# x @ w_in by Strassen's seven block products behind the first 512 tokens, weights' operands streamed from scratch memory

## The chip, the core and the metric

One core of a Trainium2 chip runs one program. The metric is the device time of that program in microseconds; "before" is the median of three runs. The engines named below are TensorE (PE, its weight loads apart as PEld), VectorE (DVE), ScalarE (ACT), GpSimd (POOL) and SyncE (SP, which here only issues DMAs). Each engine works through its own instructions in the order in which they were written; engines meet through semaphores.

## What is computed

```python
def _attn_ref(q, k, v):                # 8 batches, 8 heads, 576 positions, 64 wide; chunks of 64
    scores = scale * np.matmul(q_c, k_c.transpose(0, 1, 2, 4, 3))
    scores = scores - np.max(scores, axis=-1, keepdims=True)
    attn = np.exp(scores)
    attn = attn / (np.sum(attn, axis=-1, keepdims=True) + 1e-09)
    out = np.matmul(attn, v_c)
...
def _moe_ref(x, w_in, w_out):          # x (4608, 512): the attention's output, all heads of a position
    h = x @ w_in                       # (512, 2048)
    sp = np.where(h > 20.0, h, np.log1p(np.exp(np.minimum(h, 20.0))))
    g = h * np.tanh(sp)
    return (g @ w_out).astype(np.float32)   # (2048, 512)
```

Attention works inside chunks of 64 positions; a feed-forward layer with the activation mish follows. The weights arrive in 64-bit floats.

## The kernel before

Tokens come in 18 pairs of two tiles (256 tokens); two pairs make a block of 512 tokens, and there are nine blocks. In each block 16 slots walk over w_in's 2048 columns, 128 at a time (f).

All wide products are made from split operands: a float32 value is kept as a high part, rounded to the format of the matmul, and a low part, the rest, and a product is low x high + high x high + high x low. `up` (L288) makes one tile h of x @ w_in, 128 columns of w_in by 512 tokens: four steps of the inner dimension 512 by three parts, 12 matmuls of 512 columns. ACT turns h into z (mish, L300); DVE, or ACT in half of the first block's slots, makes the parts gh and gl (L308, L306, L313); `down` (L326) multiplies them with w_out's parts into four accumulators for 128 tokens each, o0 (tokens 0 to 255) and o2 (256 to 511), again 12 matmuls. At the end of a block `store` copies the accumulators to ob on ACT (L340) and DVE (L338) in turn, three buffers for four copies, and SP writes them out (L344).

PE's order is written out by hand in `slot(s)`: `up` of slot s+1, a step of attention if the plan has one, `down` of slot s-1. Attention of a pair (scores s and values av, L162; transposes pt, L231; maximum, subtraction, sum and norm on DVE, L189, L201, L215, L222; exp and copies on ACT, L210, L241) runs a block ahead, one step a slot; its output x is split straight from the accumulator into xh (ACT, L262) and xl (DVE, L265).

The weights are split during the first block. Each 128-row piece is loaded by SP (wis, wos, L82), made into float32 by two ACT passes (L89, L93) and two DVE passes (L99), and split by an ACT copy (L114) and a DVE subtraction (L117). w_in's and w_out's parts then stay on the chip to the end. A prologue does the first two pairs in halves, and the first pieces of the weights.

## Time and profile before

| | |
|---|---|
| median of three runs | 878.55 us (878.55 to 880.42) |
| span of the profiled execution | 876.5 us |
| median less that span | 2.05 us |
| PE busy | 854.2 us, 97% of the span |
| DVE busy | 342.8 us |
| ACT busy | 254.2 us |
| moved by DMA | 55.40 MB |

In rows of groups stand the line, engine and operation, output <- inputs, the shape and the count, then the busy time in all and the mean of one in ns, then the engine's idle time before them and what ended it. In rows of the timeline and of the chain the first number is the start and the second the duration, both in us. Instructions overlap at their edges on DVE, ACT and PE, so starts lie a little closer than durations say. An instruction that waits for its operands stands as idle time of its engine, in brackets.

### The profile page before, as it was taken

To read this page: it belongs to the slowest core of one execution; us is meant where nothing else is said; L and a number is where in the kernel's file an instruction comes from. 1 tells how busy PE (TensorE), PEld (TensorE's weight loads), DVE (VectorE), ACT (ScalarE), POOL (GpSimd) and SP (SyncE) were. 2 spreads that over 40 slices of the span, in tenths; PEclk is the share of its full clock that TensorE was granted. 3 is DMA by queue.
4 is the path that set the end of the run, shared out by engine and by line. 5 is a ranking of instruction groups with operands and counts; after the bars stand their busy time and mean duration, and the time that the engine had idled before them with its cause. 6 is when DMAs were issued, how large, how long until landed. Compare 5 with 4: busy or idle time off the path is not lost.

```text
span 876.5 us, 13523 instructions
## 1 busy us (share of the span) xinstructions
PE 854.2 (97%) x5916; PEld 703.9 (80%) x5916; DVE 342.8 (39%) x534; ACT 254.2 (29%) x360; POOL 0.7 (0%) x6
## 2 busy tenths in 40 slices
PE   4999999999999999999999999999999999999996
PEld 4778888888888888888888888888888888888885
DVE  6899845242334233323424242423242243322221
ACT  4888832121312122221213131212222131321111
POOL 0000000000000000000000000000000000000000
PEclk9899999999999999999999999999999999999999
DMA  7657512101210120112120121013101211001002
GB/s 264 204 183 251 180 36 62 49 25 49 73 49 25 49 73 25 49 31 60 31 73 7 42 73 49 25 49 73 39 35 49 52 37 57 0 6 43 1 1 48
DMA packets 25179, 55.40 MB, mean 63 GB/s; under 512 B 2592, under 2 KB 2592, under 8 KB 25120
## 3 DMA queue, kind: packets, MB, share of 16 engines
q1 hardware_dynamic: 24832, 54.01, 20.5%
q8 instruction: 46, 0.75, 0.4%
q10 hardware_dynamic: 288, 0.52, 0.2%
q14 instruction: 13, 0.11, 0.0%
HBM read 45.09 MB, written 9.44 MB: 62 GB/s over the span
## 4 chain that ended last, share of the span: by engine, by line
PE 91%; DVE 4%; ACT 3%; issue 1%; DMA 1%; SPq 0%; DVEq 0%; ACTq 0%
PE o L326 43%; PE h L288 41%; PE av L162 2%; PE s L162 2%; PE pt L231 2%; DVE wic L99 1%; DVE woc L99 1%; DVE m L189 1%; DVE wo_l L117 0%; DMA k<-in_k 0%; ACT L300 0%; DVE p L222 0%; DVE p L201 0%; ACT L210 0%; ACT woc L89 0%
## 5 line engine op out<-in xcount | busy, mean ns | idle before, releaser
L308 DVE CAST gh<-z 128x512 fp32r<-128x512 f32 x136 | 57.9, 426 | 453.4 <-PE o L326 453.4
L326 PE MATMUL o<-wo_h,gl 128*128 128x512 f32 x576 | 229.0, 398 | 0.0
L326 PE MATMUL o<-wo_h,gh 128*128 128x512 f32 x576 | 224.5, 390 | 0.0
L326 PE MATMUL o<-wo_l,gh 128*128 128x512 f32 x576 | 224.5, 390 | 0.0
L300 ACT ACTIVATE z<-h 128x512 f32<-128x512 f32 x144 | 86.2, 599 | 451.4 <-PE h L288 345.6
L288 PE MATMUL h<-xh,wi_l 128*128 128x512 f32 (+1 forms) x580 | 154.9, 389 | 0.7 <-ACT xh L262 0.7
L288 PE MATMUL h<-xl,wi_h 128*128 128x512 f32 (+1 forms) x580 | 155.2, 390 | 0.0
L288 PE MATMUL h<-xh,wi_h 128*128 128x512 f32 (+1 forms) x580 | 154.7, 389 | 0.0
L288 PEld LDWEIGHTS h<-xh,wi_l 128*128 128x128 f32 x580 | 108.9, 189 | 23.3 <-ACT xh L262 0.9
L288 PEld LDWEIGHTS h<-xl,wi_h 128*128 128x128 f32 x580 | 109.2, 190 | 22.4
L288 PEld LDWEIGHTS h<-xh,wi_h 128*128 128x128 f32 x580 | 109.1, 189 | 22.4
L326 PEld LDWEIGHTS o<-wo_h,gl 128*128 128x128 f32 x576 | 108.1, 188 | 23.1
L326 PEld LDWEIGHTS o<-wo_h,gh 128*128 128x128 f32 x576 | 108.1, 188 | 22.8
L326 PEld LDWEIGHTS o<-wo_l,gh 128*128 128x128 f32 x576 | 108.2, 188 | 21.1
L313 DVE TENSOR_TENSOR gl<-z,gh 128x512 fp32r<-128x512 f32 x144 | 99.6, 692 | 9.7 <-ACT gh L306 5.0
L241 ACT COPY ps<-pt 128x1024 f32<-128x1024 f32 (+1 forms) x20 | 18.6, 931 | 83.8 <-PE pt L231 83.8
L338 DVE COPY ob<-o 128x512 f32<-128x512 f32 x18 | 12.5, 692 | 53.8 <-ACT ob L340 30.9
L300 ACT ACT_TABLE_LOAD x17 | 21.8, 1283 | 34.5 <-PE h L288 34.5
L231 PE MATMUL pt<-ident,p 128*128 128x128 f32 x144 | 20.0, 282 | 9.3 <-ACT wis L93 5.9
L231 PEld LDWEIGHTS pt<-ident,p 128*128 128x128 f32 x144 | 17.0, 144 | 12.9 <-issue 6.0
L162 PEld LDWEIGHTS s<-k,q 64*64 64x64 f32 x1088 | 18.3, 139 | 11.0 <-issue 5.6
L162 PE MATMUL s<-k,q 64*64 64x64 f32 x1088 | 20.8, 227 | 5.3 <-DMA k<-in_k 5.3
(36 smaller groups left out, 370.6 us busy)
## 6 DMA issues: line engine op xcount, KB each, us to landing
out<-ob SPq DMA_DIRECT2D x72, 128.0 KB, 2.4
wis<-in_w_in SPq DMA_DIRECT2D x16, 512.0 KB, 3.6
wos<-in_w_out SPq DMA_DIRECT2D x16, 512.0 KB, 3.9
q<-in_q SPq DMA_DIRECT2D x16, 512.0 KB, 3.7
k<-in_k SPq DMA_DIRECT2D x16, 512.0 KB, 3.5
v<-in_v SPq DMA_DIRECT2D x16, 512.0 KB, 3.9
room_v<-in_v SPq DMA_DIRECT2D x2, 512.0 KB
k<-in_k ACTq DMA_DIRECT2D x2, 256.0 KB
```

The lines of the kernel that those rows point to most:

```text
L99: nc.vector.scalar_tensor_tensor(out=c, in0=x, scalar=mask, in1=d["a"][:, :, 0] if op == ALU.logical_shift_left else c, op0=op, op1=ALU.bi ...
L162: nc.tensor.matmul(o[h * CHUNK : (h + 1) * CHUNK, c, t - ts.start, g], lhsT=l[rows, t, 2 * g + h], rhs=r[rows, t, 2 * g + h], start=True, ...
L189: nc.vector.tensor_reduce(out=small(j, "m", t), in_=st[j]["s", t.start].rearrange("p c t g k -> p c (t g) k"), op=ALU.max, axis=AX.X,)
L231: nc.tensor.transpose(out=d["pt", ts.start][:, t - ts.start, g], in_=d["p"][:, t, g].rearrange("p c k -> p (c k)"), identity=ident,)
L241: nc.scalar.copy(out=d["ps"][:, t].rearrange("p t h k -> p (t h k)"), in_=d["pt", t.start][:, : t.stop - t.start].rearrange("p t g n -> p ...
L288: nc.tensor.matmul(h[:, cols], lhsT=w_[:, f, kt], rhs=x[:, kt, cols], start=(n == 0), stop=(n == 3 * NK - 1),)
L300: nc.scalar.activation(out=d["z"], in_=d["h"], func=AF.Mish)
L308: nc.vector.tensor_copy(out=d["gh"], in_=d["z"])
L313: nc.vector.tensor_tensor(out=d["gl"], in0=d["z"], in1=d["gh"].bitcast(F32), op=ALU.subtract)
L326: nc.tensor.matmul(acc[t], lhsT=g[:, sl], rhs=w_[:, f], start=(f == 0 and n == 0), stop=(f == NF - 1 and n == 2),)
L338: nc.vector.tensor_copy(out=o, in_=acc[t])
```

## The change

The first block of 512 tokens is computed as before. The other 16 pairs are taken in four quads of 1024 tokens, and x @ w_in in each of them goes by seven block products (Strassen's method, in a form with fewer sums). For unit u of eight, columns 256u to 256u+255 of w_in, transposed, are cut into four blocks of 128 columns by 256 inner rows, A11, A12 (first 128 columns) and A21, A22; x of the quad into B11, B12, B21, B22, 256 inner rows by 512 tokens. The sums are S1 = A21 + A22, S2 = S1 - A11, S3 = A11 - A21, S4 = A12 - S2 and T1 = B12 - B11, T2 = B22 - T1, T3 = B22 - B12, T4 = B21 - T2. Each product has two inner steps and three parts, 6 matmuls. Where two results share products, one accumulator is copied out by ACT midway (x to z, b1, b2) and goes on accumulating; the rest is added by DVE (`add`, L656 of the changed kernel).

The parts of the seven A operands are not kept on the chip. In the first block the float32 pieces of w_in are written to scratch memory (cs), and so are the parts of A11, A12 and A22 (ra). The parts of the S are made once, unit by unit: `s_load` reads cs back into a tile bld, `s_build` makes four sums on DVE, their high parts on ACT and the low ones on DVE, and SP stores them (sa). This is done in slots 14 and 15 and at six places of quad 1's units 0 to 3. From there every product's operand, 256 KB, is loaded by SP (`load_op`), six ahead. The attention's output is copied to raw tiles, and the parts of B and T come from these (`x_sums`, `x_split`), for the first quad in slots 9 to 15.

A quad has two halves. In the first, eight units make h; tokens of pairs 0 and 2 are activated, split and fed to `down` at once, those of pairs 1 and 3 stay as b1 and b2 (zb). `down` now only appends its 24 matmuls a unit to a list, from which the next unit takes three or five behind each product (`filled`). In the second half the list is filled from zb, 24 matmuls a tick for eight ticks. The first block carries attention for four pairs instead of two; a quad carries that of the next four pairs, on 32 ticks.

```diff
--- before.py
+++ after.py
@@ stores of the weights operands, in the weight steps
+    raw_ops = [dram.tile([P, 3, 2, 256], F32, name=f"ra_{u}") for u in range(NU)]
+    sum_ops = [dram.tile([P, 4, 2, 256], F32, name=f"sa_{u}") for u in range(NU)]
+    w_c = [dram.tile([P, 2, DM], F32, name=f"cs_{u}") for u in range(NU)]
...
+        if m == "i":
+            nc.sync.dma_start(out=w_c[f // 2][:, f % 2], in_=c.bitcast(F32))
...
+    def w_keep(n):
+        m, f = order[n]
+        if m == "i":
+            t = wi[f].bitcast(F32).rearrange("p s (a k) c -> p s a (k c)", a=2)
+            u = f // 2
+            if f % 2 == 0:
+                for a in range(2):
+                    nc.sync.dma_start(out=raw_ops[u][:, a], in_=t[:, :, a])
+            else:
+                nc.sync.dma_start(out=raw_ops[u][:, 2], in_=t[:, :, 1])
...
+    def s_load(u):
+        if "t" not in bld:
+            bld["t"] = zb_p.tile([P, 16 * 256], F32, name="bld", tag="z")
+        t = bld["t"]
+        nc.sync.dma_start(
+            out=t[:, 0 : 2 * DM], in_=w_c[u].rearrange("p h c -> p (h c)")
+        )
+    def s_build(u):
+        t = bld["t"]
+        a = t[:, 0 : 2 * DM].rearrange("p (n c) -> p n c", c=256)
+        s = t[:, 2 * DM : 4 * DM].rearrange("p (n c) -> p n c", c=256)
+        o = t[:, 4 * DM :].rearrange("p (n s c) -> p n s c", s=2, c=256)
+        a11, a12, a21, a22 = (a[:, n] for n in range(4))
+        s2, s1, s3, s4 = (s[:, n] for n in range(4))
+        for out_, x, y, op in (
+            (s1, a21, a22, ALU.add),
+            (s2, s1, a11, ALU.subtract),
+            (s3, a11, a21, ALU.subtract),
+            (s4, a12, s2, ALU.subtract),
+        ):
+            nc.vector.tensor_tensor(out=out_, in0=x, in1=y, op=op)
+        nc.scalar.copy(out=o[:, :, 0].bitcast(F32R), in_=s)
+        nc.vector.tensor_tensor(out=o[:, :, 1].bitcast(F32R), in0=s, in1=o[:, :, 0], op=ALU.subtract)
+        nc.sync.dma_start(out=sum_ops[u], in_=o)
@@ the operands of x
+    def x_split(m, half, *names):
+        for name in names:
+            src = raw_half(m, half, name)
+            hi = x_half(m, half, name, 0)
+            nc.scalar.copy(out=hi, in_=src)
+            nc.vector.tensor_tensor(
+                out=x_half(m, half, name, 1), in0=src, in1=hi.bitcast(F32), op=ALU.subtract
+            )
+    def x_sums(m, half):
+        for out_, x, y in (
+            ("T1", "B12", "B11"),
+            ("T3", "B22", "B12"),
+            ("T2", "B22", "T1"),
+            ("T4", "B21", "T2"),
+        ):
+            nc.vector.tensor_tensor(
+                out=raw_half(m, half, out_),
+                in0=raw_half(m, half, x),
+                in1=raw_half(m, half, y),
+                op=ALU.subtract,
+            )
@@ w_out as a list of single matmuls
-    def down(i):
...
+    def down(key, f, d):
+        for t in range(TOK // P):
+            for n in range(3):
+                fill.append((key, f, d, t, n))
+    def filled(n=None):
+        for _ in range(len(fill) if n is None else min(n, len(fill))):
+            down_mm(*fill.pop(0))
@@ slot(s), s < 16 only
+        if s == 9:
+            x_split(1, 0, "B11", "B21")
+        if s == 10:
+            x_split(1, 0, "B22")
+        if s == 11:
+            x_sums(1, 0)
+        if s == 12:
+            x_split(1, 0, "T2", "T3", "T1")
+        if s == 14:
+            x_split(1, 0, "T4")
+            x_split(1, 1, "B11", "B21", "B22")
+            s_load(0)
+            s_build(0)
+            for i in range(LOOK):
+                load_op()
+        if s == 15:
+            x_sums(1, 1)
+            x_split(1, 1, "T2", "T1", "T3", "T4")
+            s_load(1)
+            s_build(1)
@@ the quads
+    LOOK = 6
+    PRODUCTS = (
+        ("A11", "B11"),
+        ("A12", "B21"),
+        ("S2", "T2"),
+        ("S1", "T1"),
+        ("S3", "T3"),
+        ("A22", "T4"),
+        ("S4", "B22"),
+    )
+    RAW = {"A11": 0, "A12": 1, "A22": 2}
+    SUM = {"S2": 0, "S1": 1, "S3": 2, "S4": 3}
+    ops = [(m, u, n) for m in range(1, QUADS + 1) for u in range(NU) for n, _ in PRODUCTS]
+    wop = []
+    def load_op():
+        if len(wop) < len(ops):
+            m, u, n = ops[len(wop)]
+            t = wop_p.tile([P, 2, 2, P], F32R, name=f"w{m}_{u}_{n}", tag="w")
+            src = raw_ops[u][:, RAW[n]] if n in RAW else sum_ops[u][:, SUM[n]]
+            nc.sync.dma_start(out=t.bitcast(F32).rearrange("p s k c -> p s (k c)"), in_=src)
+            wop.append(t)
+    def product(m, u, n, o, start):
+        t = wop[((m - 1) * NU + u) * len(PRODUCTS) + n]
+        x = [xo[PRODUCTS[n][1], part] for part in range(2)]
+        i = 0
+        for w_, x_ in ((0, 0), (1, 0), (0, 1)):
+            for kt in range(2):
+                nc.tensor.matmul(
+                    o,
+                    lhsT=t[:, w_, kt],
+                    rhs=x[x_][:, kt],
+                    start=(start and i == 0),
+                    stop=(i == 5),
+                    skip_group_check=not start,
+                )
+                i += 1
+        load_op()
...
+    BUILD = {0: 2, 2: 3, 4: 4, 6: 5, 8: 6, 10: 7}
+    def build(m, tick):
+        if m == 1 and tick in BUILD:
+            s_load(BUILD[tick])
+            s_build(BUILD[tick])
+    def unit(m, u):
+        tick = 3 * u
+        if u % 4 == 0:
+            zb[u // 4] = zb_p.tile([P, 4, 2, TOK], F32, name=f"zb_{m}_{u}", tag="z")
+        b1, b2 = (zb[u // 4][:, u % 4, n] for n in range(2))
+        a1, a2 = {"z": z_tile(f"z_{m}_{2 * u}")}, {}
+        x = ps_h.tile([P, TOK], F32, name=f"x_{m}_{u}", tag="h")
+        product(m, u, 0, x, True)
+        filled(3)
+        nc.scalar.copy(out=a1["z"], in_=x)
+        on_tensor(m, tick)
+        y = ps_h.tile([P, TOK], F32, name=f"y_{m}_{u}", tag="h")
+        product(m, u, 1, y, True)
+        filled(5)
+        add(y, a1["z"])
+        mish(a1["z"], a1["z"])
+        build(m, tick)
+        beside(m, tick)
+        product(m, u, 2, x, False)
+        filled(3)
+        nc.scalar.copy(out=b1, in_=x)
+        on_tensor(m, tick + 1)
+        y = ps_h.tile([P, TOK], F32, name=f"v_{m}_{u}", tag="h")
+        product(m, u, 3, y, True)
+        filled(5)
+        g_split(a1, a1["z"], f"{m}_{2 * u}")
+        build(m, tick + 1)
+        beside(m, tick + 1)
+        product(m, u, 4, x, False)
+        filled(3)
+        nc.scalar.copy(out=b2, in_=x)
+        on_tensor(m, tick + 2)
+        filled(2)
+        product(m, u, 5, x, False)
+        add(y, b2)
+        a2["z"] = z_tile(f"z_{m}_{2 * u + 1}")
+        mish(a2["z"], x)
+        product(m, u, 6, y, False)
+        filled()
+        mish(b2, b2)
+        add(y, b1)
+        mish(b1, b1)
+        g_split(a2, a2["z"], f"{m}_{2 * u + 1}")
+        build(m, tick + 2)
+        beside(m, tick + 2)
+        down((m, 0), 2 * u, a1)
+        down((m, 0), 2 * u + 1, a2)
...
+    def phase_two(m):
+        after = m < QUADS
+        p = first_pair(m)
+        for i in range(NU):
+            tick = 3 * NU + i
+            on_tensor(m, tick)
+            filled()
+            if i == 0:
+                store(f"{m}a", (p, p + 2))
+            for f in (2 * i, 2 * i + 1):
+                d = {}
+                g_split(d, z_of(f), f"{m}b_{f}", True)
+                down((m, 1), f, d)
+            beside(m, tick)
+            if after:
+                if i == 0:
+                    x_split(m + 1, 0, "B11", "B21", "B22")
+                if i == 1:
+                    x_sums(m + 1, 0)
+                    x_split(m + 1, 0, "T2", "T1", "T3", "T4")
+                if i == 4:
+                    x_split(m + 1, 1, "B11", "B21", "B22")
+                if i == 5 and m + 1 < QUADS:
+                    load_qk(first_pair(m + 2))
+                if i == 5:
+                    x_sums(m + 1, 1)
+                    x_split(m + 1, 1, "T2", "T1", "T3", "T4")
...
-        for s in range(N + 1):
+        for s in range(NF):
             slot(s)
+        for m in range(1, QUADS + 1):
+            for u in range(NU):
+                unit(m, u)
+                if u == 0:
+                    if m == 1:
+                        store("0", (0, 1))
+                    else:
+                        p = first_pair(m - 1)
+                        store(f"{m - 1}b", (p + 1, p + 3))
+            phase_two(m)
+        filled()
+        p = first_pair(QUADS)
+        store("last", (p + 1, p + 3))
```

The places in the new order on which the prediction rests are these. First DVE, from the end of slot 14 into the first unit (x_B and x_T are parts of the operands of x, raw their source; z the first result's tile):

```order
L372 TENSOR_TENSOR x_B_1_1305<-raw_1513,x_B_0_1303 128x4x2x64 [waits Activation_49]
L195 TENSOR_TENSOR bld<-bld 128x256 [waits DMAHW6_49]
...
L197 TENSOR_TENSOR bld<-bld 128x4x256 [waits Activation_49]
...
L372 TENSOR_TENSOR x_T_1_1438<-raw_1513,x_T_0_1436 128x4x2x64 [waits Activation_49]
L372 TENSOR_TENSOR x_T_1_1556<-raw_1288,x_T_0_1554 128x4x2x64 [waits Activation_49]
L195 TENSOR_TENSOR bld<-bld 128x256 [waits DMAHW0_49]
...
L197 TENSOR_TENSOR bld<-bld 128x4x256 [waits DMAHW7_49,Activation_49]
L656 TENSOR_TENSOR z_0_1614<-y_0_1628,z_0_1614 128x512 [waits PE_49,Activation_49]
L195 TENSOR_TENSOR bld<-bld 128x256 [waits DMAHW4_49,DVE_49]
```

All of these rows are new. Each build stands in DVE's queue with a wait for a DMA at its head, and the first add of the unit behind two of them.

SP's queue at the same place (ra, sa and cs are the scratch tensors, w_ a product's operand, in_q and in_k the next pair's input):

```order
L178 DMA bld<-cs_116 128x1024 [waits DMAHW6_49,PE_49]
L198 DMA sa_108<-bld 128x2048 [waits DMAHW7_49,DVE_49]
L635 DMA w_0_A_1573<-ra_100 128x512 [waits DMAHW0_49]
L635 DMA w_0_A_1575<-ra_100 128x512 [waits DMAHW1_49]
L635 DMA w_0_S_1577<-sa_108 128x512 [waits DMAHW7_49,DMAHW2_49]
...
L209 DMA q_1589<-in_q 128x2x512 [waits DMAHW6_49]
L209 DMA k_1590<-in_k 128x2x512
L178 DMA bld<-cs_117 128x1024 [waits DMAHW0_49]
L198 DMA sa_109<-bld 128x2048 [waits DMAHW1_49,DVE_49]
```

The store of each build and the loads of the first operands and of the next pair's input stand ahead of the next build's load.

Then the end of an output block. Before, DVE's two copies stood between splits of gh and gl of the next block, and PE had this between the last matmul into one block's accumulators and the first into the next one's:

```order
L326 MATMUL o_2_481<-wo_h,gh_1304 128x512
L288 MATMUL h_1361<-xl_858,wi_h 128x512 [waits Activation_49]
L288 MATMUL h_1361<-xl_858,wi_h 128x512 x3
L288 MATMUL h_1361<-xh_857,wi_h 128x512 x4
L288 MATMUL h_1361<-xh_857,wi_l 128x512 x4
L162 MATMUL s_0_1374<-k_1311,q_1310 64x64 [waits DMAHW1_49,DMAHW0_49,PE_49]
L162 MATMUL s_0_1374<-k_1311,q_1310 64x64 x31
L326 MATMUL o_0_1407<-wo_h,gl_1341 128x512 [waits DVE_49]
```

Now, between the two halves of quad 1, PE has only a step of attention in between:

```order
L435 MATMUL o_(1, 0)_2_1820<-wo_l,gh_15_2825 128x512
L435 MATMUL o_(1, 0)_2_1820<-wo_h,gh_15_2825 128x512
L294 MATMUL pt_0_2895<-ident,p_2784 128x128 [waits DVE_49,PE_49,Activation_49]
L294 MATMUL pt_0_2895<-ident,p_2784 128x128 x7
L435 MATMUL o_(1, 1)_0_2904<-wo_h,gl_1b_2876 128x512 [waits Activation_49]
L435 MATMUL o_(1, 1)_0_2904<-wo_l,gh_1b_2874 128x512 [waits Activation_49]
```

and DVE, in front of that transpose's operand p:

```order
L456 COPY ob_1a_2862<-o_(1, 0)_0_1803 128x512 [waits Activation_49]
L456 COPY ob_1a_2870<-o_(1, 0)_2_1820 128x512 [waits DMAHW1_49,DMAHW0_49,Activation_49]
L424 TENSOR_TENSOR gl_1b_2876<-zb_0_1613,gh_1b_2874 128x512 [waits Activation_49]
L424 TENSOR_TENSOR gl_1b_2880<-zb_0_1613,gh_1b_2878 128x512 [waits Activation_49]
L285 TENSOR_TENSOR p_2784<-p_2784,r_0_2830 128x2x8x64 [waits DVE_49]
```

The twelve matmuls of h that stood there are gone; the transposes stand ahead of the first matmul into the new accumulator, and the norm of p behind the copies and two splits.

## The prediction

> **What bounds the kernel now.** I read the page's busy times first, then the chain that ended last, then the busy time by stage.

> ```profile
> span 876.5 us, 13523 instructions
> PE 854.2 (97%) x5916; PEld 703.9 (80%) x5916; DVE 342.8 (39%) x534; ACT 254.2 (29%) x360; POOL 0.7 (0%) x6
> ...
> 135.96 2.72 PE h L288 x12
> 138.68 2.72 PE o L326 x12
> ```

> PE is busy 97% of the span, and the chain is a string of groups of twelve matmuls, for x @ w_in (h) and g @ w_out (o) in turn, each 2.72 us: 0.227 us for a matmul of 512 columns. The only thing that shortens such a kernel is fewer matmuls, as long as PE never waits.

> ```profile
> 22.00:110.00 88.00, 84.53 (x668) 69.34 (x666) 79.48 (x126) 74.80 (x122) 0.00 (x0) 0.96 0.63 204
> ...
> 200.00:870.00 670.00, 669.54 (x4457) 551.46 (x4456) 213.80 (x330) 145.25 (x191) 0.00 (x0) 1.00 0.14 40
> ```

> In these rows by stage (PE, PEld, DVE, ACT, POOL, clock, DMA share, GB/s) there are two regimes. From 200 us on PE is busy 669.5 of 670 us and DVE a third of it. In the first block, where the weights are split, DVE is busy 79.5 of 88 us and ACT 74.8: little room there. The change puts its extra elementwise work into that block and right behind it.

> **Term 1, the matmuls removed: -43.5 us.** For two rows of 128 of w_in and 1024 tokens, 4 x 12 = 48 matmuls become 7 products of 6, 42. Eight such units in each of four quads: 32 x 6 = 192 fewer, x 0.227 = 43.5 us. All of it is on PE, which sets the end.

> **Term 2, the first block: +4 us (0 to 12).** The block of 16 slots now carries attention for four pairs instead of two, four of the sums T, and six of the splits of x.

> ```profile
> L189 DVE TENSOR_REDUCE m<-s 128x16 f32<-128x1024 f32 x16 | 19.5, 1218 | 0.0
> L222 DVE TENSOR_TENSOR p<-p,r 128x1024 f32<-128x1024 f32 x16 | 19.5, 1219 | 0.0
> L265 DVE TENSOR_TENSOR xl<-av,xh 128x1024 fp32r<-128x1024 f32 x16 | 19.5, 1218 | 0.0
> L313 DVE TENSOR_TENSOR gl<-z,gh 128x512 fp32r<-128x512 f32 x144 | 99.6, 692 | 9.7 <-ACT gh L306 5.0
> L216 DVE TENSOR_SCALAR r<-r 128x16 f32<-128x16 f32 x16 | 2.8, 175 | 0.5
> L217 DVE RECIPROCAL r<-r 128x16 f32<-128x16 f32 x16 | 4.1, 254 | 0.6
> ```

> A pair costs DVE four passes of 1.22 us and 0.43 us of small ones, 5.3 us; the subtraction into xl (1.22 us a pair) is gone. So +2 x 5.3 - 2 x 1.22 + (4 + 6) x 0.69 = +15.1 us, and DVE goes from 79.5 to 94.6 us. PE takes two more pairs there (moved, not new): at 6% of the span for 18 pairs (the shares of s, pt and av in the chain below) 2.9 us each, 84.5 + 5.8 = 90.3.

> ```profile
> PE 91%; DVE 4%; ACT 3%; issue 1%; DMA 1%; SPq 0%; DVEq 0%; ACTq 0%
> PE o L326 43%; PE h L288 41%; PE av L162 2%; PE s L162 2%; PE pt L231 2%; DVE wic L99 1%; DVE woc L99 1%; DVE m L189 1%; DVE wo_l L117 0%; DMA k<-in_k 0%; ACT L300 0%; DVE p L222 0%; DVE p L201 0%; ACT L210 0%; ACT woc L89 0%
> ```

> DVE now needs 4 us more than PE. None of it shows if PE's lag of a slot absorbs it; 12 if DVE's 8.5 us of idle stay on top.

> **Term 3, eight operand builds at the head of DVE's queue: +30 us (16 to 45).** Each build starts with a load from scratch memory issued right ahead of it, so DVE waits out the landing; then four sums of 256 columns, an ACT copy of 1024, and a DVE pass of 1024.

> ```profile
> wis<-in_w_in SPq DMA_DIRECT2D x16, 512.0 KB, 3.6
> out<-ob SPq DMA_DIRECT2D x72, 128.0 KB, 2.4
> ...
> L241 ACT COPY ps<-pt 128x1024 f32<-128x1024 f32 x16 | 16.3, 1017 | 79.4 <-PE pt L231 79.4
> ```

> The landing is a load of 512 KB, 3.6 us. 256 columns are not in the trace: from 0.69 us for 512 and 1.22 for 1024, 0.53 per 512, so about 0.42. A build is 4 x 0.42 + 1.02 + 1.22 = 3.9 us, 7.5 with its landing. Behind a waiting build on DVE stand the adds that free the accumulators (add of y before the fourth product, of b2 before the seventh), the gh and gl of the next fill, and the copies of finished outputs; on ACT, the copy of x before the third and fifth product. PE waits for each. Adding up DVE's hundred rows from gl of slot 13 through the eighth build, at these durations, gives 64 us; with ACT's eight copies 72.5; with eight landings of 3.6, 101. PE has 230 matmuls (52.1 us) and four steps of attention (4.4) in that stretch, 56.5. So PE loses 16 us if every landing is hidden, 45 if none is. The first is hidden behind three splits and the last ones in part; but the store of 1 MB (sa) stands between each build and the next load on SP's queue. I take the middle, 30.

> **Term 4, nothing between two accumulations: +32 us (18 to 36).** Today a block's end is covered:

> ```profile
> 126.48 2.72 PE o L326 x12
> ...
> 127.88 0.59 ACT L340 COPY ob<-o 128x512 f32<-128x512 f32 x1 [0.43 <-PE o L326]
> 128.50 0.69 DVE L338 COPY ob<-o 128x512 f32<-128x512 f32 x1 [3.11 <-ACT ob L340]
> 129.24 0.59 ACT L340 COPY ob<-o 128x512 f32<-128x512 f32 x1 [0.77 <-PE o L326]
> 131.85 1.16 PE L162 MATMUL s<-k,q 64*64 64x64 f32 x64
> 132.27 0.69 DVE L338 COPY ob<-o 128x512 f32<-128x512 f32 x1 [3.08 <-DMA out<-ob]
> 132.94 0.50 PE L326 MATMUL o<-wo_h,gl 128*128 128x512 f32 x1
> ```

> The last matmul of the old output ends its turn at T = 129.0; the fourth copy waits until an earlier copy's buffer has been written out, T + 3.2, and is done at T + 3.9. PE needs no accumulator until 132.94, because twelve matmuls of h and the scores lie between. After the change a quad's first half ends with 24 fills, and the second begins with a transpose and 24 fills. DVE's order is: fourth copy (T + 3.9), gl, gl (0.61 us apart, T + 5.1), the norm (1.22, T + 6.3), splits. PE's transposes stand ahead of its fills and wait for that norm: idle 6.3 us, three times. In quad 4 no pair is left, and fills start at T + 4.6.

> ```profile
> L210 ACT ACT_TABLE_LOAD x17 | 21.8, 1283 | 1.9 <-PEq L512 1.7
> L210 ACT ACTIVATE p<-p 128x1024 f32<-128x1024 f32 x16 | 17.0, 1061 | 0.2
> L300 ACT ACTIVATE z<-h 128x512 f32<-128x512 f32 x144 | 86.2, 599 | 451.4 <-PE h L288 345.6 <-issue 105.6
> ```

> At the other turn (after the first unit of a quad) only one product, 1.36 us, covers. ACT does mish (0.6), a table load (1.28), exp (1.06) and the copy (0.59) from 0.05 on: 3.6; DVE waits for exp, sums and inverts (1.6, at 4.6), and copies (5.3). 5.3 - 1.36 = 4.0, twice; 0.9 in quad 4; quad 1's is in term 3. Sum 3 x 6.3 + 4.6 + 2 x 4.0 + 0.9 = 32. If output buffers never made the fourth copy wait, about 18; with one more microsecond in each, 36.

> **Term 5, splits in the second half: +8 us (0 to 11).** Sums and four splits stand ahead of the next gl in DVE's queue, 8 x 0.69 = 5.5 us against 5.4 of fills (24 x 0.227). gl then comes 1.9 us late, and a values step waits as long for ACT; twice in three quads is 11. I take 8, since the preceding tick lends some room.

> In the steady units I add nothing. ACT and DVE do 7 and 6 passes in 15 us of PE; the shortest cover is the five fills (1.13 us) between the fifth and sixth product, against a copy of 0.59. Streaming 7 x 256 KB a unit is 115 GB/s beside the row that moved 398:

> ```profile
> 10.00:12.00 2.00, 1.09 (x4) 1.00 1.03 398
> ```

> With six loads in flight an operand has 12 us to land, against 3.6.

> **Term 6, the clock: +12 us (0 to 37).**

> ```profile
> 18.00:24.00 6.00, 2.35 (x22) 1.00 0.00 1
> 24.00:26.00 2.00, 1.80 (x64) 0.58 0.16 55
> 26.00:28.00 2.00, 1.49 (x7) 0.50 0.96 314
> 28.00:30.00 2.00, 2.00 (x9) 0.50 0.96 275
> 30.00:32.00 2.00, 2.00 (x8) 0.71 1.04 416
> ```

> (PE busy, clock, DMA share, GB/s.) After six microseconds with PE busy 2.35, the granted clock was halved for about 6.8 us: 3.4 us lost. Term 4 has six stalls of 4 us or more, and term 3's 30 us would be some five such; all eleven with a drop would be 37 us. I take a third. [...]

> **Sum.** -43.5 + 4 + 30 + 32 + 8 + 12 = +42.5, a span of 919. The median of the runs shown (878.55) lies 2.05 above the span, so **921 us**. All low ends give 869, all high ones 976.

> **Rivals.** *The gain is kept* (faster): landings are hidden and the copies finish before PE asks, so that only 16 us of builds and about 14 at the boundaries stay: -43.5 + 16 + 14 = -13.5, 865 us. For it: steady units are covered, and the trace's own boundary has PE waiting for nothing. Against: that cover was twelve matmuls that no longer stand there. It decides if the builds cost under 16 and a boundary under 2 us. *Every stall halves the clock* (slower still): 37 instead of 12 gives 946. For it: the drop above came after pauses of at most 2.5 us. Against: it is the only one. *The streamed operands are late*: each product would wait 3.6 - 2.1 us, 224 times, 336 us, some 1170 us in all; the 398 GB/s speak against it. *A draw*: the two sums meet within 0.3%, about what a measurement of this kernel can tell from no change, near 878.

> **Chances.** Forecast 0.57, halved clock 0.20, gain kept 0.17, draw 0.04, late operands 0.02. So faster 0.17, same 0.04, slower 0.79. The forecast's own range is 890 to 945. With the unknowns of terms 3 and 6 and the draw the range is 876 to 956, which leaves out the kept gain and the late operands.

> **What would show it.** Right, if the 512-column matmuls number 192 fewer, still 0.227 us apart; if PE's waits name the bld and add lines, the norm ahead of pt, and the ob copies; if stages of three steady units show PE over 98% busy; and if the stretch from slot 14 to unit 3 is some 30 us longer than its matmuls. Wrong, if PE is busy all through the quads' turns, or if DVE does not idle at bld for a landing.

## Result and the profile after

The changed kernel takes **982.68 us** (median of four runs, 980.88 to 983.48), against 878.55 before: a ratio of 1.118, 95% interval 1.116 to 1.120. Slower was forecast, but 921 us, with 956 as the upper end.

The page of the changed kernel, the rows that answer to those shown of before:

```profile
span 981.6 us, 14157 instructions
PE 854.0 (87%) x5724; PEld 690.9 (70%) x5724; DVE 439.5 (45%) x678; ACT 381.3 (39%) x584; POOL 0.7 (0%) x6
...
PEclk9899996778899989999999899999998999999999
```

192 matmuls are gone, as worked out, and yet TensorE is busy as long as before (854.0 against 854.2 us), in a span that is 105.1 us longer. Two things did this. It pauses: span less busy time is 127.6 us, before 22.3. And it works at half clock: the row PEclk has dips where it had one.

The busy time by stage (us, then PE, PEld, DVE, ACT, POOL, clock, DMA share, GB/s; the first two rows are units 0 to 3 of quad 1, the third units 4 to 7, the fourth quad 1's second half, which begins with the turn between the halves, and the last seven units of quad 4):

```profile
139.90:198.40 58.50, 24.89 (x137) 18.89 (x136) 29.04 (x49) 17.16 (x26) 0.00 (x0) 0.75 0.55 184
198.40:270.80 72.40, 52.53 (x312) 40.89 (x313) 28.25 (x46) 19.50 (x27) 0.00 (x0) 0.85 0.57 178
270.80:349.70 78.90, 78.68 (x577) 63.95 (x577) 29.02 (x44) 28.39 (x41) 0.00 (x0) 0.98 0.51 154
349.70:421.00 71.30, 62.40 (x377) 50.66 (x376) 32.92 (x50) 25.43 (x42) 0.00 (x0) 0.93 0.24 63
...
815.70:925.60 109.90, 109.33 (x480) 89.96 (x480) 32.01 (x52) 29.76 (x51) 0.00 (x0) 1.00 0.42 113
```

The steady units do what they should: 109.33 of 109.90 us busy at full clock. The loss lies at the start of the first quad, where PE is busy 77 of 131 us at a clock of 0.75 and 0.85, and at each turn. No engine is full there: DVE is busy 57 of those 131 us, ACT 37. It is a matter of order.

PE's own rows of the timeline at the start (in brackets the pause ahead and what ended it), and then one turn between halves, the second half behind it, and the turn into the next quad:

```profile
152.79 2.90 PE L644 MATMUL x<-x_B,w_A 128*128 128x512 f32 x6 [12.88 <-DMA w_A<-ra]
165.68 2.93 PE L644 MATMUL x<-x_T,w_S 128*128 128x512 f32 x6 [5.35 <-ACT z L706]
177.81 2.93 PE L644 MATMUL x<-x_T,w_S 128*128 128x512 f32 x6 [4.53 <-ACT zb L718]
198.42 0.79 PE L435 MATMUL o_(1, 0)_0_1803<-wo_h,gl 128*128 128x512 f32 x1 [10.88 <-DVE ob L456]
217.46 1.99 PE L226 MATMUL av<-ps,v 64*64 64x64 f32 x64 [5.95 <-ACT ps L304]
...
270.76 1.51 PE L294 MATMUL pt<-ident,p 128*128 128x128 f32 x6 [7.67 <-DVE p L285]
355.16 1.94 PE L294 MATMUL pt<-ident,p 128*128 128x128 f32 x8 [5.44 <-DVE p L285]
365.62 1.16 PE L226 MATMUL av<-ps,v 64*64 64x64 f32 x64 [1.62 <-ACT ps L304]
396.06 0.50 PE L435 MATMUL o_(1, 1)_0_2904<-wo_h,gl_1b 128*128 128x512 f32 x1 [1.85 <-DVE gl_1b L424]
425.14 0.79 PE L435 MATMUL o_(2, 0)_0_3383<-wo_h,gl 128*128 128x512 f32 x1 [4.08 <-DVE ob_1b L456]
```

With three smaller ones (2.90, 2.60, 0.58) the pauses from 140 to 271 us come to 53.3 us. The turns come to 28.7 (5.44 and twice 5.45; 3.62 and 0.61 in quad 4; 4.08 at the start of quads 2 and 3), the second halves to 10.4, the first block to 12.9, before 1.6. Behind the start stand these waits of DVE, the rows of SP's queue, and the DMA rows (KB, then median us from issue to landing):

```profile
DVE bld L195 <- DMA bld<-cs: 34.0, 7, 9.1
DVE bld L197 <- ACT bld L196: 9.2, 8, 1.2
...
147.13 0.32 SPq L198 DMA_DIRECT2D sa<-bld  x1
147.50 1.40 SPq L635 DMA_DIRECT2D w_A<-ra  x2
152.03 1.27 SPq L635 DMA_DIRECT2D w_S<-sa  x3
...
154.80 0.67 SPq L178 DMA_DIRECT2D bld<-cs  x1
...
sa<-bld SPq DMA_DIRECT2D x8, 1024.0 KB, 4.9
...
bld<-cs SPq DMA_DIRECT2D x8, 512.0 KB, 5.0
```

A build's load is written right ahead of the build, so nothing covers it: SP comes to it behind the store of the build before and the operands' loads that follow (those of S operands, w_S, wait until that store has landed). Build 1's was issued at 154.80, 1.4 us after DVE began to wait, and landed 7.6 us later. Of DVE's 34.0 us, 3.9 lie ahead of the issue (builds 1 and 2); the other 30.1 lie between issue and landing, which took 5.0 us in the median, where a 512 KB load of before took 3.6. The first operands, which need no build at all, stand in SP's queue behind build 0's store, issued at 147.13 when DVE was done, and landed 5.2 us after their own issue: 12.88 us for PE.

The clock: the changed kernel has twenty stretches at half clock, the last of them behind PE's last matmul. Five of them and the sum row (us of the stretch, then columns as above):

```profile
22.08:32.32 10.24, 8.50 (x87) 7.43 (x88) 7.32 (x12) 8.36 (x14) 0.00 (x0) 0.50 0.63 213
...
110.83:114.24 3.41, 3.41 (x11) 2.73 (x9) 3.23 (x7) 2.15 (x5) 0.00 (x0) 0.50 0.90 279
...
353.17:360.00 6.83, 4.84 (x16) 4.20 (x17) 3.65 (x6) 0.00 (x0) 0.00 (x0) 0.50 0.45 119
397.55:400.96 3.41, 3.41 (x9) 2.64 (x8) 0.00 (x0) 0.60 (x1) 0.00 (x0) 0.50 0.00 0
424.85:428.26 3.41, 3.12 (x7) 2.48 (x8) 0.93 (x2) 0.68 (x1) 0.00 (x0) 0.50 0.74 171
...
sum 113.02, PE 80.92 PEld 65.73 DVE 52.01 ACT 30.14 POOL 0.00; mean PE 4.05 PEld 3.29 DVE 2.60 ACT 1.51 POOL 0.00
```

PE worked 80.9 us in them, so about half of that, 40.5 us, was lost. (Matmuls of 512 columns start 0.43 us apart there, at 397.98, 398.41 and 398.84 for one, against 0.227; by that spacing it is 38 us. The count by half is used throughout.) Before, the same count is:

```profile
sum 9.07, PE 6.12 PEld 5.47 DVE 5.32 ACT 6.62 POOL 0.00; mean PE 3.06 PEld 2.73 DVE 2.66 ACT 3.31 POOL 0.00
```

3.1 us. With that the difference of the spans, by its definition, splits into three: pauses 127.6 - 22.3 = +105.3; half clock 40.5 - 3.1 = +37.4; and PE's work at full clock (854.0 - 40.5 = 813.5, before 854.2 - 3.1 = 851.1) -37.6. Sum +105.1.

### The profile page after: what moved, and what is told of

Read it like the earlier page. It is cut to its first block, busy times and chain, and to the rows that moved or that the text cites. A ratio compares the mean times of both kernels' runs of the same rounds, so it can differ in the third digit from the quotient of the medians.

```text
span 981.6 us, 14157 instructions
## 1 busy us (share of the span) xinstructions
PE 854.0 (87%) x5724; PEld 690.9 (70%) x5724; DVE 439.5 (45%) x678; ACT 381.3 (39%) x584; POOL 0.7 (0%) x6
## 4 chain that ended last, share of the span: by engine, by line
PE 65%; DVE 13%; ACT 7%; DMA 7%; issue 3%; SPq 1%; ACTq 0%; DVEq 0%
PE x L644 16%; PE v L644 8%; PE y L644 4%; DMA bld<-cs 3%; PE o_(4, 1)_0_7181 L435 2%; PE o_(4, 0)_0_6431 L435 2%; PE o_(4, 1)_2_7188 L435 2%; PE o_(1, 1)_0_2904 L435 2%; PE o_(3, 1)_0_6000 L435 2%; PE o_(2, 1)_0_4452 L435 2%; PE o_(4, 0)_2_6448 L435 2%; PE o_(1, 1)_2_2911 L435 2%; PE o_(2, 1)_2_4459 L435 2%; PE o_(3, 1)_2_6007 L435 2%; PE o_(3, 0)_0_4931 L435 2%
## 5 line engine op out<-in xcount | busy, mean ns | idle before, releaser
L644 PE MATMUL x<-x_T,w_S 128*128 128x512 f32 x384 | 102.7, 404 | 16.0 <-ACT zb L718 8.0
L656 DVE TENSOR_TENSOR zb<-v,zb 128x512 f32<-128x512 f32 x64 | 44.2, 690 | 126.4 <-PE v L644 94.8
L644 PEld LDWEIGHTS x<-x_T,w_S 128*128 128x128 f32 x384 | 74.3, 195 | 33.5 <-ACT zb L718 9.3
L644 PE MATMUL x<-x_B,w_A 128*128 128x512 f32 x192 | 50.8, 401 | 12.9 <-DMA w_A<-ra 12.9
L424 DVE TENSOR_TENSOR gl<-z,gh 128x512 fp32r<-128x512 f32 x80 | 55.4, 693 | 9.8 <-ACT gh L420 7.4
L644 PE MATMUL y<-x_B,w_A 128*128 128x512 f32 x192 | 53.6, 418 | 0.0
L656 DVE TENSOR_TENSOR z<-y,z 128x512 f32<-128x512 f32 x32 | 22.1, 690 | 69.7 <-PE y L644 69.7
L402 PE MATMUL h<-x_first,wi 128*128 128x512 f32 (+1 forms) x204 | 51.4, 407 | 0.7 <-ACT x_first L334 0.7
L644 PE MATMUL x<-x_T,w_A 128*128 128x512 f32 x192 | 50.8, 401 | 0.0
L644 PE MATMUL v<-x_T,w_S 128*128 128x512 f32 x192 | 50.5, 398 | 0.1
L644 PE MATMUL v<-x_B,w_S 128*128 128x512 f32 x192 | 49.0, 391 | 0.0
L644 PEld LDWEIGHTS x<-x_T,w_A 128*128 128x128 f32 x192 | 37.6, 196 | 8.4
## 6 DMA issues: line engine op xcount, KB each, us to landing
wst<-in_w_in SPq DMA_DIRECT2D x16, 512.0 KB, 5.8
wst<-in_w_out SPq DMA_DIRECT2D x16, 512.0 KB, 5.7
q<-in_q SPq DMA_DIRECT2D x16, 512.0 KB, 4.0
k<-in_k SPq DMA_DIRECT2D x16, 512.0 KB, 5.6
v<-in_v SPq DMA_DIRECT2D x16, 512.0 KB, 4.5
```

The lines of the kernel that those rows point to most:

```text
L402: nc.tensor.matmul(h[:, cols], lhsT=wi[i][:, w_, kt], rhs=x[:, x_, kt, cols], start=(n == 0), stop=(n == 3 * NK - 1),)
L424: nc.vector.tensor_tensor(out=d["gl"], in0=z, in1=d["gh"].bitcast(F32), op=ALU.subtract)
L644: nc.tensor.matmul(o, lhsT=t[:, w_, kt], rhs=x[x_][:, kt], start=(start and i == 0), stop=(i == 5), skip_group_check=not start,)
L656: nc.vector.tensor_tensor(out=z, in0=o, in1=z, op=ALU.add)
```

## Experiments

Theory A: the eight builds at the head of DVE's queue make the pauses at the start. Theory B: the rest is the turns, each with a named instruction that comes too late. Theory C: a pause costs a second time, by the clock. The rivals stand in the expectations. All ratios are to the kernel before, in the same runs; pauses are span less PE's busy time, and half clock is the time lost by the count above, both from the one profiled execution of each kernel, which lies up to 3.5 us off the median. In e6 the added matmuls count as busy.

| run | median us | ratio (95%) | pauses us | half clock us |
|---|---|---|---|---|
| before | 878.55 | 1 | 22.3 | 3.1 |
| changed | 982.68 | 1.118 (1.116 to 1.120) | 127.6 | 40.5 |
| e1, no builds | 926.17 | 1.054 (1.052 to 1.057) | 79.6 | 27.5 |
| e2, loads earlier | 952.56 | 1.084 (1.083 to 1.086) | 103.7 | 31.0 |
| e4, norm first | 971.57 | 1.106 (1.104 to 1.108) | 119.0 | 36.5 |
| e5, four output buffers | 970.68 | 1.105 (1.102 to 1.109) | 119.2 | 36.5 |
| e7, output copies first | 975.29 | 1.111 (1.109 to 1.113) | 120.0 | 35.5 |
| e6, idle matmuls | 976.66 | 1.112 (1.110 to 1.114) | 109.4 | 33.3 |
| e9, builds on GpSimd | 953.46 | 1.085 (1.083 to 1.088) | 108.7 | 29.7 |
| e8, all moves | 901.26 | 1.026 (1.023 to 1.028) | 66.5 | 16.9 |
| e10, e8 without builds | 873.06 | 0.995 (0.993 to 0.996) | 45.9 | 12.3 |
| e11, e8, seven builds on GpSimd | 889.38 | 1.013 (1.011 to 1.015) | 57.0 | 11.8 |
| e12, e11, S of unit 0 direct | 888.97 | 1.013 (1.010 to 1.016) | 60.0 | 12.0 |
| e13, e12, build 0 on DVE | 894.92 | 1.018 (1.017 to 1.020) | 59.7 | 14.4 |

### e1: no builds

```diff
-            src = raw_ops[u][:, RAW[n]] if n in RAW else sum_ops[u][:, SUM[n]]
+            src = raw_ops[u][:, RAW[n] if n in RAW else SUM[n] % 3]
...
-            s_load(0)
-            s_build(0)
```

(and the other seven calls). The S operands are read from the stored parts of A11, A12 and A22 in their place, so the same bytes are streamed, but the kernel leaves out the sums S, and its h is not x @ w_in.

> Leaves out the eight builds (the sums S and their parts are never made; the four S operands are read from the scratch copies of A11, A12 and A22 instead, so the same number of bytes is streamed). Theory A (the builds at the head of DVE's queue make the stalls from slot 14 to unit 3, and each stall also halves the clock for a while): of the 53 us of PE's idle time in that stretch about 45 go, and of the 20 us lost there to the halved clock about 18: 983 - 63 = about 920 us. Theory B (the stretch is slow because of the splits of x, the attention and the output copies, which are all still there): at least 960 us.

It took 926.17 us, near what theory A expected and 56.5 less than the changed kernel: 48.0 us of pauses and 13.0 of half clock went. Of the pauses of the first units only 0.28, 3.10 and 4.08 us stayed. The start is the builds' doing; but even without them the kernel is 48 us slower than before, by the turns, the first block and the clock.

### e2: the next build's load ahead of this build's store

```diff
             nc.vector.tensor_tensor(out=out_, in0=x, in1=y, op=op)
+        if u + 1 < NU:
+            s_load(u + 1)
         nc.scalar.copy(out=o[:, :, 0].bitcast(F32R), in_=s)
...
-            s_load(1)
             s_build(1)
```

> Only the place of the load changes: the load for build u+1 is issued as soon as build u's four sums have read the tile, ahead of the store of build u, instead of right before build u+1. DVE waited 34 us for these landings in all. Theory A1 (the landing at the head of DVE's queue is what costs): DVE's wait at bld falls under 8 us and the time by about 30 us, 953. Theory A2 (the build's own passes on DVE and ACT and the waits of SP's queue cost as much without it): 970 or more.

30.1 us came off. DVE's waits for the builds' loads, and what was left of PE's:

```profile
DVE bld L195 <- DMA bld<-cs: 3.5, 1, 3.5
...
152.81 2.90 PE L645 MATMUL x<-x_B,w_A 128*128 128x512 f32 x6 [12.57 <-DMA w_A<-ra]
182.22 0.80 PE L437 MATMUL o_(1, 0)_0_1804<-wo_h,gl 128*128 128x512 f32 x1 [7.20 <-DVE ob L458]
```

34.0 us of landings became 3.5, by where one issue stands in a queue. The first pause, operands behind build 0's store, did not move.

### e4, e5 and e7: the turns

e4 puts the norm ahead of the output copies at the turn between halves; e5 gives the copies a fourth buffer (and the operands five in place of six); e7 puts the copies of the old output ahead of the third tick's build and attention in a quad's first unit.

```diff
e4 (the norm of that tick leaves `beside`)
             if i == 0:
+                if pair_at(m, tick, 2) is not None:
+                    a_norm(pair_at(m, tick, 2))
                 store(f"{m}a", (p, p + 2))
e5
-    c_p = ctx.enter_context(tc.tile_pool(name="c", bufs=3))
+    c_p = ctx.enter_context(tc.tile_pool(name="c", bufs=4))
...
e7 (the call moved here from behind unit 0)
+        if u == 0:
+            if m == 1:
+                store("0", (0, 1))
+            else:
+                p = first_pair(m - 1)
+                store(f"{m - 1}b", (p + 1, p + 3))
         build(m, tick + 2)
         beside(m, tick + 2)
```

> At the turn between a quad's halves the norm is put ahead of the output copies on DVE; nothing else moves. If PE's 5.45 us there is the chain copy, wait for the written buffer, copy, gl, gl, norm, transposes, then the transposes now run at once and PE waits for the fourth copy and gl instead, T + 4.6: 2.0 to 2.8 us less at each of three turns, 975 to 977 us. If the wait is for the accumulator's buffer alone, it stays within 2 us of 983.

> Four output buffers instead of three (and, for room, five streamed operands in flight instead of six), so that the fourth output copy of a turn needn't wait for a written buffer. If that wait is part of the chain at the halves' turn, DVE has its copy at T + 0.9 instead of T + 3.9, PE's 5.45 us fall to about 3 in quads 1 to 3 and its 3.6 to about 1.5 in quad 4, and less of the clock is lost: 970 to 976 us. If the operands are late with five in flight, PE's waits name w_A or w_S and it is slower than 983.

> At the other turn the output copies stand ahead of the third tick's build, exp and inverse instead of behind them. If these stand in the way, PE's 4.08 us before the first fill of unit 1 fall to about 0.6 in quads 2 and 3 (with the half clock behind them, 1.5 each) and 10.9 to about 3 in quad 1: about 18 us less, 965. If the copies wait for their written buffers or for the accumulator itself, 980 or more.

11.1, 12.0 and 7.4 us came off, in e4 somewhat more than expected. Rows of e4 (what is left of a turn), of e5, and of e7 (quad 1's third product):

```profile
354.35 0.50 PE L435 MATMUL o_(1, 1)_0_2904<-wo_h,gl_1b 128*128 128x512 f32 x1 [1.76 <-DVE gl_1b L424]
```

```profile
351.17 1.94 PE L294 MATMUL pt<-ident,p 128*128 128x128 f32 x8 [3.83 <-DVE p L285]
```

```profile
201.96 2.93 PE L644 MATMUL x<-x_T,w_S 128*128 128x512 f32 x6 [9.90 <-ACT z L706]
```

In e4 the 5.44 us became 0.81 and 1.76, in e5 3.83: both halves of the turn's arithmetic, the norm's place and the buffer that the fourth copy waits for, are real. In e7 4.08 became 0.61 in quads 2 and 3, but in quad 1 the 10.88 us in front of the output matmul only came out one product later, as 9.90, behind ACT's copy: the engine was late, not the instruction. So e7 gave 7.4 us, where about 18 were expected and the three pauses that it was after have 19.0.

### e6: work that keeps the clock

84 matmuls without a use are put ahead of the transposes at the turns (24 in quads 1 to 3, 12 in quad 4).

```diff
+            if i == 1:
+                idle_work(24 if m < QUADS else 12)
             on_tensor(m, tick)
```

> Adds work: at the turn between a quad's halves PE does 24 matmuls (5.4 us, 12 of them in quad 4) on constant operands into an accumulator that nobody reads, ahead of the transposes, where it stood idle 5.45 us (3.6). Theory C (each idle stretch of this length is followed by PE at half the granted clock, apart from the idle time itself): the half clock behind the turn (4.8 us of PE work at 0.5, 2.4 us lost in quads 1 to 3, 1.7 in quad 4, perhaps the same again behind the next short stall) is gone, 973 to 976 us with 84 matmuls more. Theory D (the low clock comes from something else, for instance from the start of the transposes or of DMA): 983 or more.

With 84 matmuls more (19 us of work) the kernel is 6.0 us faster, 0.7 us above the range of theory C and 6 us below theory D. The turn, two rows that lay at 0.54 and 0.50 in the changed kernel:

```profile
353.00:355.00 2.00, 2.00 (x10) 1.68 (x9) 0.45 (x1) 2.00 (x5) 0.00 (x0) 1.00 0.90 207
355.00:357.00 2.00, 2.00 (x10) 1.65 (x10) 2.00 (x4) 0.49 (x1) 0.00 (x0) 1.00 0.86 200
```

The order of everything else at the turn is as it was, so this shows that the clock's part of a pause is a cost of its own. Half-clock time fell from 40.5 to 33.3 us, 7.2.

### e8: all moves together

e2, e4, e5 and e7, and four more: the first two operands are loaded ahead of build 0's store, the T splits go on two ticks, builds 3, 4 and 7 come a tick later, and in a second half's second tick the copy of pt stands ahead of gh.

```diff
             s_load(0)
+            load_op()
+            load_op()
             s_build(0)
...
-    BUILD = {0: 2, 2: 3, 4: 4, 6: 5, 8: 6, 10: 7}
+    BUILD = {0: 2, 3: 3, 5: 4, 6: 5, 8: 6, 11: 7}
```

> All repairs of the order together: the build loads ahead (as in e2), the first two operands loaded ahead of the first build, builds of quad 1 at ticks 0, 3, 5, 6, 8 and 11, the norm ahead of the copies (e4), four output buffers (e5), the copies ahead of the third tick's exp (e7), and in the second half the T splits spread over two ticks and the copy of pt ahead of gh. If stalls and half clock are all there is, the separate gains add up: 30 (e2) + 11 (e4) + 7 (e7) + about 8 (e5) + 10 (second half) + 5 = 71, 912 us. If the stalls only move on, as quad 1's did in e7, 940 or more.

901.26 us, 11 better than expected. 61.1 us of pauses and 23.6 of half clock went; e2, e4, e5 and e7 alone had taken 48.5 and 22.5, so the rest of the pauses is the share of the moves that were not run alone, or of their meeting. One large pause stays, ahead of the first product with an S operand:

```profile
155.60 2.93 PE L647 MATMUL x<-x_T,w_S 128*128 128x512 f32 x6 [10.47 <-ACT z L708]
```

Two things can be behind it, build 0's round trip through scratch memory, and T2 behind ACT's and DVE's work for the builds; e12 and e13 go after both.

### e9: the builds on GpSimd

All passes and transfers of the builds are written for GpSimd (`nc.gpsimd` in `s_load` and `s_build`), nothing else is moved.

> The eight builds go, passes and DMAs alike, to POOL and its queue, which have nothing else to do; DVE, ACT and SP lose them. Theory A: what PE lost was DVE's and ACT's place in line, so it comes out near the kernel without builds (926), within 15 us above it for the first operands that still come late. Theory A3 (it is the sums' own latency that PE waits for, wherever they are made): 960 or more, with PE waiting for w_S loads.

953.46 us, 29 us less than the changed kernel, between what the two theories expected (up to 941, or 960 and more). The rows of GpSimd and of PE's two large pauses:

```profile
L195 POOL TENSOR_TENSOR bld<-bld 128x256 f32<-128x256 f32 x32 | 24.9, 800 | 48.8 <-DMA bld<-cs 48.2
L197 POOL TENSOR_TENSOR bld<-bld 128x1024 fp32r<-128x1024 f32 x8 | 19.4, 2420 | 0.6
...
158.65 2.90 PE L644 MATMUL x<-x_T,w_S 128*128 128x512 f32 x6 [12.46 <-DMA w_S<-sa]
255.89 2.93 PE L644 MATMUL x<-x_T,w_S 128*128 128x512 f32 x6 [13.04 <-ACT zb L718]
```

GpSimd takes twice DVE's time for a pass (0.80 against 0.42 us, 2.42 against 1.22) and waits 48 us for its loads; the last build ends too late, and unit 4's tile zb, which takes the build's memory, waits for it.

### e10 and e11: what the products are worth

e10 is e8 without the builds (S operands as in e1, so its h is not x @ w_in either), e11 is e8 with builds 1 to 7 on GpSimd, their loads ahead of the stores.

> All moves of the run with everything together (loads of the first operands first, norm and output copies moved ahead, four output buffers, splits spread over two ticks), and none of the eight builds: the S operands are read from the stored A columns in their place, so S2, S1, S3 and S4 are not computed. It asks what the seven products are worth here when their operands cost nothing. The run with everything and the builds took 901.3 us, with 33.8 us of TensorE's work at half clock and some 24 us of pauses between 140 and 271 us. Theory A (the builds alone still hold those pauses): pauses at the start fall to about 5 us, half-clock work to about 20 us, so 901 - 19 - 7 = 875 us, about the time of the kernel before (878). Theory B (the pauses at the start belong to the switch itself, the first operands' landings and the attention there): at least 890 us.

> The run with everything together (901.3 us), with the builds of units 1 to 7 moved, passes, copies and transfers, to GpSimd, each load ahead of the store of the build before; build 0 stays on VectorE and ScalarE. GpSimd needs about 8.5 us for each (four sums of 0.8, a cast of 1.1, a subtraction of 2.4, and the landing it can't hide), so all seven end before about 200 us, ahead of unit 4 that needs their tile. Theory A (the pauses at the start are VectorE's and ScalarE's queues behind the builds): most of the 24 us of pauses there go, and some 5 us of half clock: 880 to 888 us. [...]

e10, with operands that cost nothing, is at 873.06 us, near theory A's 875, ratio 0.995: of 43.5 us of removed matmuls some 5 are left, since 23.6 us of pauses and 9.2 of half clock over the kernel before stay even there. e11 is at 889.38, just above the range of its theory A: 12 of the 28 us between e8 and e10. Its remaining large pause stands where e8's does, 9.72 us, now on the load of S2.

### e12 and e13: the first S operand

In e12 unit 0 loads its S operands from the build's own tile, all builds are on GpSimd, and q and k of the next pair are asked for earlier. In e13 build 0 is back on DVE and ACT, behind the T sums, and GpSimd starts after it.

```diff
-            src = raw_ops[u][:, RAW[n]] if n in RAW else sum_ops[u][:, SUM[n]]
+            src = raw_ops[u][:, RAW[n]] if n in RAW else (bld["o"] if (m, u) == (1, 0) else sum_ops[u])[:, SUM[n]]
```

> The run with units 1 to 7 built on GpSimd took 889.4 us and keeps three pauses at the start: 9.72 us (the first S operand, which goes from the build's tile to scratch memory and back), 2.42 (q and k of the next pair, asked for late) and 1.22. Here unit 0's S operands are loaded from the build's own tile, without the way through scratch memory; its store goes out behind them; build 0 is on GpSimd too, the builds 1 to 7 are issued behind unit 0's second product, and q and k are asked for ahead of build 0. Theory A (the round trip through scratch memory and VectorE's queue made the 9.72): that pause falls to about 4 us, 2.42 goes, half-clock work falls by some 5 us: 878 to 882 us. Theory B (T2's sums and splits end no earlier, so the wait only changes hands): 886 us or more.

> The run with all builds on GpSimd and unit 0's S operands straight from the build's tile took 889.0 us and still has a pause of 9.43 us ahead of the product of S2 and T2, now on T2: while GpSimd's sums and passes of build 0 ran (141 to 150 us), VectorE's subtractions for the T sums took 2.02 and 2.71 us, against 0.63 and 0.69 where GpSimd was idle. Here build 0 goes back to VectorE and ScalarE, its sums behind the T sums, and GpSimd starts only with the load of build 1, which waits in SyncE's queue behind the S operands' loads and build 0's store. Theory A (VectorE and GpSimd slow each other, and that kept T2 late): the T sums are back at about 0.7 us each, T2 and S2 are there by about 151 us, the pause is about 6 us and the time 883 to 886 us. Theory B (T2 was late for another reason): the sums are no faster or the pause stays above 8 us, and the time at 888 us or more.

e12 came to 888.97, no gain, as theory B had it: the pause is 9.43 us, now on ACT's copy and T2. GpSimd and DVE in e12:

```profile
140.90 4.03 POOL L198 TENSOR_TENSOR bld<-bld 128x256 f32<-128x256 f32 x4 [3.06 <-DMA bld<-cs]
146.95 2.67 POOL L202 TENSOR_TENSOR bld<-bld 128x1024 fp32r<-128x1024 f32 x1
...
145.40 2.02 DVE L390 TENSOR_TENSOR raw<-raw,raw 128x512 f32<-128x512 f32 x1
147.46 2.71 DVE L390 TENSOR_TENSOR raw<-raw 128x512 f32<-128x512 f32 x1
```

The same two sums in e13, where GpSimd is idle until 160.61, and PE's pauses there:

```profile
142.93 0.68 DVE L393 TENSOR_TENSOR raw<-raw,raw 128x512 f32<-128x512 f32 x1
143.65 0.69 DVE L393 TENSOR_TENSOR raw<-raw 128x512 f32<-128x512 f32 x1
...
152.10 2.90 PE L653 MATMUL x<-x_T,w_S 128*128 128x512 f32 x6 [5.87 <-DMA w_S<-bld]
...
178.27 1.65 PE L653 MATMUL x<-x_T,w_S 128*128 128x512 f32 x6 [3.59 <-DMA w_S<-sa]
```

The sums are back at 0.68 and 0.69, and the pause at 5.87, both as theory A said. The time is not: 894.92, 6 us above e12. GpSimd now starts on build 1 ten microseconds later and unit 1's S operands are late in turn (3.59 us), so that the pauses come to as much as in e12 (59.7 and 60.0 us), and half clock to 2.4 us more. What makes the rest of the 6 us is not shown. No version with the builds beat the kernel before; e12 and e11, at 1.013, are the nearest.

## Why the prediction was right and wrong

The direction and the places were right; the size was off by 62 us, in three terms.

**Term 1 (-43.5), the matmuls: right in count, 37.6 in PE's time.** 192 fewer, and a steady unit of quad 4 (861.54 to 876.50 us) takes 14.96, which is 66 x 0.227. Why PE's work at full clock fell by 5.9 us less than the count says was not tested; e10, with 815.5 us of work, is no nearer. The way of counting offers most of it: a matmul's record lasts 0.39 us, but the next one starts 0.227 behind it, so each pause leaves 0.16 us more that counts as busy. PE's records have 43 gaps between them, before 8: an estimate of 35 x 0.16 = 5.7 us.

**Term 2 (+4, up to 12): 11.** The pauses of the first block went from 1.6 to 12.9 us, at the upper end of the range. PE's lag did not absorb DVE's extra work: the two largest, 3.27 and 2.78 us, end with the norm of p on DVE. The loads were slower too, 5.8 us for 512 KB, where 3.6 was the row of before; what part of the pauses they made is not shown.

```profile
wst<-in_w_in SPq DMA_DIRECT2D x16, 512.0 KB, 5.8
```

**Term 3 (+30, 16 to 45), the builds: 53, above the range.** The step that failed is "the landing is a load of 512 KB, 3.6 us", with about half of the landings taken as hidden. Only build 0's was hidden; the other seven took 4.1 to 7.6 us from issue to landing, and DVE waited 34.0 us for them, 4.9 each and up to 9.1, more than the 29 us that eight landings made in the worst case. The text named the store on SP's queue and put no price on it, and the first operands behind it (12.88 us) were in no term at all. The old output's copies behind DVE's build (10.88) were meant to be within the 30. e2 shows the first part: 30 us by moving one issue; e1 shows the whole, 56.5 us with the half clock.

**Term 4 (+32, 18 to 36), the turns: 28.7.** 6.3 was 5.45, 4.6 was 3.62, 4.0 was 4.08, 0.9 was 0.61. The same instructions as named (e4, e5).

**Term 5 (+8): 10.4**, 1.62 and 1.85 us in each of three quads. Nothing for the steady units: right.

**Term 6 (+12, 0 to 37), the clock: 37.4.** "I take a third" failed. The one drop in the trace of before came after pauses of up to 2.5 us, and it was taken for a rare thing; in the changed kernel it follows 19 of 23 pauses of 1.8 us or more. There were nineteen stretches with work in them, not eleven, at 2.1 us each, not 3.4. The rival "every stall halves the clock" had nearly the right rule, and a chance of 0.20; that its price (37) was right too is luck, too few stalls times too high a cost. As a term it belonged in the forecast. What one pause costs differs: one of 1.85 us was followed by a half-clock stretch of 3.41 us, 1.7 us lost (397.55 in the rows above), one of 5.44 us by a stretch of 6.83 us, 2.4 us lost (353.17).

With 11, 53.3 and 37.4 in place of 4, 30 and 12 the same sum gives 921 + 56 = 977 us. So the way of adding up holds; the builds and the clock were mis-sized by 23 and 25 us, and the misses of terms 1, 4 and 5 (+5.9, -3.3 and +2.4) make up most of the rest.

## What to carry to other kernels

In this kernel 19 of TensorE's 23 waits of 1.8 us or more cost their length plus, on average, some 2 us of half clock (40.5 us in 19 stretches), and the three of 1.62 us their length alone; price an unhidden wait with both parts. Where a loop loads, computes and stores through one queue, ask when the queue comes to the load, how long the load takes beside the other traffic (5.0 us here and not 3.6), and what covers it; moving the next load ahead of the store took 30 us here. A saving of 5% on a kernel that keeps its bound engine 97% busy must come with new work that needs no place on the path: even with free operands 5 of 43 us were left.

## What the runs showed of the hardware

Work without a use can pay: e6's 84 matmuls filled room that pauses had, and the time fell by 6 us.

VectorE's passes were slower while GpSimd worked: 2.02 and 2.71 us in e12, beside GpSimd's passes up to 149.62 us, against 0.68 and 0.69 in e13, where GpSimd was idle, for the same two sums of 512 columns. These sums have two inputs; the copies to gh, which have one, were slowed too, to 2.42 us in e13 (165.95) and 1.41 in e12 (162.07) from 0.42 (e13, 149.51). Not every pass was: VectorE's adds with one input in an accumulator took 0.68 and 0.69 us beside GpSimd's passes (e13, 162.61 and 165.20), as they did elsewhere (0.69 in the mean of the changed kernel's 96). GpSimd's own passes were 0.80 us for 256 columns and 2.42 for 1024 in e9, where VectorE took 0.42 and 1.22 in the changed kernel.
